# Result stores on SyncE's queue, streamed weights on GpSimd's, and the next pair's conversion placed behind the operands it follows

## The chip, the core and the metric

The kernel runs on one core of one Trainium2 chip. The metric is the time of one execution on the device in microseconds. Before the change it is 922.56 us, the median of three runs (919.75 to 926.53).

## What is computed

Local attention over chunks of 64 tokens, in fp32, and a feed-forward layer with a PReLU on its output; q, k, v are 8 x 8 x 576 x 64, so there are 4608 tokens of width 512, and the hidden width is 2048.

```python
scores = scale * np.matmul(q_c, k_c.transpose(0, 1, 2, 4, 3))      # chunks of 64 tokens
attn = np.exp(scores - np.max(scores, axis=-1, keepdims=True))
attn = attn / (np.sum(attn, axis=-1, keepdims=True) + 1e-09)
x = merge_heads(np.matmul(attn, v_c))                               # 4608 x 512
h = x @ w_in                                                        # 4608 x 2048
g = np.maximum(h, 0.0) + alpha * np.minimum(h, 0.0)
out = g @ w_out                                                     # 4608 x 512
```

## The kernel before

Every fp32 matmul is made of three passes of a reduced format (fp32r): each operand is split into a high part (a cast on ScalarE) and a low part (a subtraction on VectorE), and high x high, high x low and low x high are summed in PSUM. `split` (L541) is that cast and subtraction.

The tokens are 36 attention pieces of 128 and 9 blocks of 512. Blocks 0 to 2 are done plainly; blocks 3 to 8 in three pairs, each by a Strassen-Winograd scheme with 7 products in place of 8.

**Attention phase with plain blocks** (steps, L440; the profile to about 382 us). 48 steps, each 24 matmuls, walk over the 16 hidden slices of blocks 0 to 2, in parts: block 0 slices 0 to 3, block 1 slices 0 to 8, then the rest of block 0, of block 1, and block 2. What a part leaves unfinished is stored as a partial sum (`store`, L350, with `keep`) and added later (L369 loads it, L370 adds it on VectorE, L383 stores the result); one buffer of two halves named "more" serves the partial sums of row blocks 0, 1 and 3, so the load for row block 3 waits until the first two results have left. In this phase the weights come in (`fetch`, L116), are split (`split_weight`, L122), and at some steps a **visit** (L402) does the scores and softmax of one attention piece and the values of an earlier one; a visit ends with eight small transfers (L242) that move VectorE's block transposes "t" into the tile pT. At every odd step from 15 to 45, `combine` (L478) forms the sums of weights that the Strassen scheme needs, on VectorE and ScalarE, and `keep_a` (L474, GpSimd's queue) writes them to HBM in tiles wi_a and wo_a.

**Pairs** (L751 on). `first_product` (L591) makes 7 products with w_in for each of 8 slices j; in pairs 0 and 1 a visit stands ahead of each j, for the blocks of the next pair. `second_product` (L647) makes 7 products with w_out (order 7, 1, 5, 6, 4, 2, 3), 8 units j each, a unit being 6 matmuls; `operand` (L624) prepares the activations of a unit, two units ahead (AHEAD, L645): a difference on VectorE where the product needs one (L628, L631), and a split (L542, L543). The weights come back from HBM by `stream` (L514): 168 loads of 512 KB, two units each, into a ring of four tiles (raw, raw, wi15, wo15); the load of a tile is issued when the tile's last matmul has been placed, so it waits for TensorE. The conversion of the next pair's activations (`convert`, L545) is 14 pieces, each a split, for four of the seven products after a difference (L560, L564); `second_product` emits one piece every four units (L682).

What sets the order: a scheduler places each instruction in the queue of its engine by a simulated timeline, program order being the priority, and lifts what stands under `tc.high_priority`; TensorE's order is pinned from step 20 on. Queues run in order, and a DMA waits in the queue of the engine that issues it. SyncE's queue (SP) issues all loads (weights, q, k, v, pT, partial sums, the stream); GpSimd's queue (POOL) issues the writes of combined weights and all result stores except the very last two.

## Time and profile before

| | |
|---|---|
| median of 3 runs | 922.56 us (919.75 to 926.53) |
| the profiled execution | 921.13 us, span 919.4 us |
| TensorE matmul busy | 838.4 us, 91% of the span |
| VectorE, ScalarE, GpSimd busy | 699.1, 539.0, 115.0 us |
| mean granted TensorE clock | 0.961 |
| DMA traffic | 184.5 MB, mean 201 GB/s; 143.2 MB of it from SP's queue, 40.4 MB from POOL's |
| stages, ends | attention phase with plain blocks 382, pair 0 574, pair 1 757, pair 2 919 |

In the lines of the profile PE is TensorE, DVE VectorE, ACT ScalarE, POOL GpSimd and SP SyncE; L524 is line 524 of the kernel; "out<-in" names the tiles; the brackets at a row's end give the time that the engine stood idle before it and what ended that. A time of "x8" rows is that of eight instructions together. Busy TensorE is not TensorE at its peak: at half clock a matmul counts as twice as long, so the granted clock is to be read beside it.

### The profile page before, as it was taken

To read this page: it belongs to the slowest core of one execution; us is meant where nothing else is said; L and a number is where in the kernel's file an instruction comes from. 1 tells how busy PE (TensorE), PEld (TensorE's weight loads), DVE (VectorE), ACT (ScalarE), POOL (GpSimd) and SP (SyncE) were. 2 spreads that over 40 slices of the span, in tenths; PEclk is the share of its full clock that TensorE was granted. 3 is DMA by queue.
4 is the path that set the end of the run, shared out by engine and by line. 5 is a ranking of instruction groups with operands and counts; after the bars stand their busy time and mean duration, and the time that the engine had idled before them with its cause. 6 is when DMAs were issued, how large, how long until landed. Compare 5 with 4: busy or idle time off the path is not lost.

```text
span 919.4 us, 15294 instructions
## 1 busy us (share of the span) xinstructions
PE 838.4 (91%) x5248; PEld 661.6 (72%) x5248; DVE 699.1 (76%) x1313; ACT 539.0 (59%) x1366; POOL 115.0 (13%) x174
## 2 busy tenths in 40 slices
PE   5798999996787899998896999899979999998998
PEld 4566888775665678876674888677758888886886
DVE  6599999987878747566689985566899845678884
ACT  5676565663554756476585643667766435565542
POOL 4013232234243200000000001000000010000000
PEclk9799999998897899999998999999999999999999
DMA  9648668566666733466664567766635676554564
GB/s 286 225 132 271 198 223 268 162 207 222 237 206 211 243 99 93 152 225 219 227 196 152 181 207 232 261 191 208 225 123 184 209 236 219 183 186 161 199 207 165
DMA packets 69212, 184.52 MB, mean 201 GB/s; under 512 B 11408, under 2 KB 18576, under 8 KB 69136
## 3 DMA queue, kind: packets, MB, share of 16 engines
q1 hardware_dynamic: 56672, 143.17, 49.1%
q0 software_dynamic: 12320, 40.38, 12.2%
q8 instruction: 42, 0.69, 0.3%
q14 instruction: 34, 0.28, 0.1%
q10 hardware_dynamic: 144, 0.01, 0.0%
HBM read 135.27 MB, written 40.89 MB: 192 GB/s over the span
## 4 chain that ended last, share of the span: by engine, by line
PE 68%; DVE 10%; DMA 9%; ACT 5%; SPq 4%; issue 3%; POOL 1%; DVEq 0%; ACTq 0%; POOLq 0%
PE ps_o L677 15%; PE ps_o L586 13%; PE ps_h L319 11%; PE ps_o L343 11%; PE ps_h L677 7%; PE ps_h L586 6%; SPq L242 2%; DMA raw<-wi_a 2%; DMA wi<-wi_a 2%; DMA wo_a<-raw 1%; DMA wi_a<-raw 1%; PE ps_a L282 1%; PE ps_a L199 1%; ACT pr L223 1%; PE ps_a L185 1%
## 5 line engine op out<-in xcount | busy, mean ns | idle before, releaser
L343 PE MATMUL ps_o<-wo,gh 128*128 128x512 f32 x384 | 116.5, 402 | 15.2 <-DVE more L370 14.5
L319 PE MATMUL ps_h<-xh,wi 128*128 128x512 f32 x384 | 112.1, 416 | 1.3 <-DVE g L311 1.3
L343 PEld LDWEIGHTS ps_o<-wo,gh 128*128 128x128 f32 x384 | 73.0, 191 | 34.0 <-DVE more L370 15.4
L319 PEld LDWEIGHTS ps_h<-xh,wi 128*128 128x128 f32 x384 | 74.0, 197 | 20.2 <-DVE g L311 1.8
L586 PE MATMUL ps_o<-wi,raw 128*128 128x512 f32 x168 | 68.2, 406 | 8.7 <-DMA raw<-wi_a 8.7
L223 ACT ACTIVATE pr<-ps_a,mx 128x64 f32<-128x64 f32 x224 | 67.0, 325 | 11.5 <-DVE mx L220 11.5
L343 PE MATMUL ps_o<-wo,gl 128*128 128x512 f32 x192 | 69.8, 397 | 0.0
L586 PE MATMUL ps_o<-wo,raw 128*128 128x512 f32 x168 | 68.0, 405 | 0.0
L663 POOL DMA_DIRECT2D outT<-xl x10 | 5.4, 541 | 454.4 <-DVE xl L653 454.1
L319 PE MATMUL ps_h<-xl,wi 128*128 128x512 f32 x192 | 54.3, 402 | 0.0
L309 ACT ACTIVATE g<-ps_h 128x512 f32<-128x512 f32 x48 | 29.0, 605 | 41.5 <-PE ps_h L319 41.0
L223 ACT ACTIVATION_READ_ACCUMULATOR pr<-ps_a,mx 128x1 f32 x224 | 48.9, 218 | 0.0
L331 ACT CAST gh<-g 128x512 fp32r<-128x512 f32 x48 | 29.8, 622 | 30.7 <-DVE g L311 18.6
L309 ACT ACTIVATE wo<-gh 128x512 f32<-128x512 f32 x24 | 15.2, 635 | 52.9 <-DVE gh L609 52.9
L542 ACT CAST gh<-wi 128x512 fp32r<-128x512 f32 x48 | 30.0, 625 | 27.3 <-PE ps_o L677 12.8
L586 PEld LDWEIGHTS ps_o<-wi,raw 128*128 128x128 f32 x168 | 32.3, 192 | 17.5 <-DVE gl L618 6.2
L319 PEld LDWEIGHTS ps_h<-xl,wi 128*128 128x128 f32 x192 | 37.6, 196 | 9.3
L343 PEld LDWEIGHTS ps_o<-wo,gl 128*128 128x128 f32 x192 | 36.4, 189 | 8.8
L504 ACT CAST raw<-t 128x512 fp32r<-128x512 f32 x32 | 19.6, 629 | 32.6 <-DVE t L500 11.1
L543 DVE TENSOR_TENSOR gl<-wi,gh 128x512 fp32r<-128x512 f32 x48 | 32.9, 685 | 7.6 <-ACT gh L542 6.9
L677 PE MATMUL ps_o<-gh,wo 128*128 128x512 f32 x112 | 38.5, 403 | 0.1
L311 DVE SCALAR_TENSOR_TENSOR g<-ps_h,g 128x512 f32<-128x512 f32 x48 | 32.6, 679 | 7.8 <-ACT g L310 7.6
(250 smaller groups left out, 2254.6 us busy)
## 6 DMA issues: line engine op xcount, KB each, us to landing
raw<-wi_a SPq DMA_DIRECT2D x42, 512.0 KB, 5.3
raw<-wo_a SPq DMA_DIRECT2D x42, 512.0 KB, 3.4
wi<-wi_a SPq DMA_DIRECT2D x21, 512.0 KB, 4.4
wo<-wi_a SPq DMA_DIRECT2D x21, 512.0 KB, 4.4
wi<-wo_a SPq DMA_DIRECT2D x21, 512.0 KB, 3.3
wo<-wo_a SPq DMA_DIRECT2D x21, 512.0 KB, 3.9
wi_a<-raw POOLq DMA_DIRECT2D x32, 256.0 KB, 4.1
wo_a<-raw POOLq DMA_DIRECT2D x32, 256.0 KB, 3.4
```

The costliest lines, as they stand in the source:

```text
L223: nc.scalar.activation(pr[:, g], one, AF.Exp, bias=mx[:, g], scale=SCALE, accum_out=sm[:, g])
L242: nc.sync.dma_start(out=pT[dst, i].rearrange("p h t -> p (h t)"), in_=tb[src, j].rearrange("p h t -> p (h t)"),)
L309: nc.scalar.activation(g, h, AF.Relu, scale=-1.0)
L311: nc.vector.scalar_tensor_tensor(g, in0=h, scalar=0.0, in1=g, op0=ALU.max, op1=ALU.subtract)
L319: pe(nc.tensor.matmul(hps, lhsT=wi[f][:, l, k * P:(k + 1) * P], rhs=xx[:, k], start=(i == 0 and k == 0), stop=(i == 2 and k == NK - 1),))
L331: nc.scalar.copy(gh, g)
L343: pe(nc.tensor.matmul(o, lhsT=a[:, ts], rhs=wo[f][:, l], start=(f == first and i == 0), stop=(f == last and i == 2),))
L504: nc.scalar.copy(w[:, 0], t)
L542: nc.scalar.copy(t_hi, t)
L543: nc.vector.tensor_tensor(t_lo, t, f32(t_hi), op=ALU.subtract)
L586: pe(nc.tensor.matmul(ps, lhsT=w[:, l, k * P:(k + 1) * P], rhs=xx[:, xl], start=first and at == 0, stop=at == n - 1, skip_group_check=not ...
L677: pe(nc.tensor.matmul(ps[m], lhsT=w[:, l, m * P:(m + 1) * P], rhs=xx, start=i != 6 and j == 0 and n == 0, stop=j == JF - 1 and n == 2, ski ...
```

## The change

Four edits. Result stores (L383, L663) all go to SP's queue, and the stream of combined weights (L524) goes to POOL's. In `second_product` a conversion piece is queued, on ScalarE and on VectorE, behind the two instructions of the split made last (`tc.issue_after` orders the queue and adds no wait). The conversion's order becomes 1, 2, 7, 5, 6, 3, 4, so that the pieces with a plain split come first, and for pair 0 its first four pieces are emitted from step 40 on. The steps at which a combine is emitted come from a table instead of every odd step. The prologue of the stream is three loads ahead of the last plain matmuls and one behind, instead of two and two.

```diff
@@ store
-            (nc.sync if end else nc.gpsimd).dma_start(out=dst, in_=ob)
+            nc.sync.dma_start(out=dst, in_=ob)
@@ stream
-        nc.sync.dma_start(out=f32(t), in_=units[side][n])
+        nc.gpsimd.dma_start(out=f32(t), in_=units[side][n])
@@ split
-        nc.scalar.copy(t_hi, t)
-        nc.vector.tensor_tensor(t_lo, t, f32(t_hi), op=ALU.subtract)
+        hi = nc.scalar.copy(t_hi, t)
+        return hi, nc.vector.tensor_tensor(t_lo, t, f32(t_hi), op=ALU.subtract)
@@ convert
-        x0, x1 = x.pop(b), x.pop(b + 1)
+        x0, x1 = x[b], x[b + 1]
...
-        order = [(i, k) for i in (7, 5, 1, 6, 3, 4, 2) for k in range(2)]
+        order = [(i, k) for i in (1, 2, 7, 5, 6, 3, 4) for k in range(2)]
@@ operand
-        split(t, hi, lo)
+        behind[:] = split(t, hi, lo)
...
+    behind = []
@@ second_product
-                (nc.sync if end and (half, col) == (0, 1) else nc.gpsimd).dma_start(out=outT[rows, cols], in_=ys[:, m])
+                nc.sync.dma_start(out=outT[rows, cols], in_=ys[:, m])
...
-                    conversion.pop(0)()
+                    with tc.issue_after(behind[0].ins), tc.issue_after(behind[1].ins):
+                        conversion.pop(0)()
@@ steps
+    COMBINE = (16, 18, 20, 21, 23, 25, 27, 28, 30, 32, 34, 36, 37, 39, 41, 43)
...
-        elif n % 2 and combined:
+        elif n in COMBINE:
...
-        if n == len(steps) - 3:
+        if n == len(steps) - 8:
             ops, conversion = convert(PLAIN)
-        if n >= len(steps) - 3:
-            for _ in range(5):
+        if n >= len(steps) - 8:
+            for _ in range(1 if len(conversion) > 10 else 0 if n < len(steps) - 3 else 4):
...
-    for _ in range(2):
+    for _ in range(3):
         stream()
...
-    for _ in range(RING - 2):
+    for _ in range(RING - 3):
         stream()
```

TensorE's order stays as it was. Three places show what moves elsewhere.

SP's queue in the first product of pair 0, at the visit whose pT transfers the trace has at 414 us; raw, wi_ and wo_ are ring tiles loaded from the combined weights wi_a. Before:

```order
L242 DMA pT<-t_4393 32x256 x8
L159 DMA q_sb<-qT 128x512
L161 DMA k_sb<-kT 128x512
L168 DMA v_sb<-v 128x512
L524 DMA raw<-wi_a_373 128x1024
L524 DMA wi_4563<-wi_a_374 128x1024
L524 DMA wo_4580<-wi_a_375 128x1024
L524 DMA raw<-wi_a_376 128x1024
L242 DMA pT<-t_4542 32x256 x8
```
After:

```order
L242 DMA pT<-t_4393 32x256 x8
L159 DMA q_sb<-qT 128x512
L161 DMA k_sb<-kT 128x512
L168 DMA v_sb<-v 128x512
L242 DMA pT<-t_4542 32x256 x8
L159 DMA q_sb<-qT 128x512
L161 DMA k_sb<-kT 128x512
```
The four stream loads between two visits are gone from SP; they stand on POOL's queue, which holds nothing but the 168 stream loads from the last written piece of combined weights to its end.

SP's queue at the end of block 0 in the attention phase; "more" and "ob" are the buffers of finished row blocks and "partial" the stored sums. Before:

```order
L242 DMA pT<-t_2125 32x256 x8
L159 DMA q_sb<-qT 128x512
L161 DMA k_sb<-kT 128x512
L168 DMA v_sb<-v 128x512
L369 DMA more<-partial_3_895 128x512
L369 DMA ob<-partial_2_1460 128x512
L242 DMA pT<-t_2299 32x256 x8
L369 DMA more<-partial_0_1452 128x512
```
After:

```order
L242 DMA pT<-t_2125 32x256 x8
L159 DMA q_sb<-qT 128x512
L161 DMA k_sb<-kT 128x512
L168 DMA v_sb<-v 128x512
L383 DMA out<-more 128x512 x2
L383 DMA out<-ob 128x512
L369 DMA more<-partial_3_895 128x512
L369 DMA ob<-partial_2_1460 128x512
L242 DMA pT<-t_2299 32x256 x8
L383 DMA out<-more 128x512
```
The three stores stood on POOL before, between writes of combined weights. They now stand on SP behind the eight pT transfers and three loads of a visit, and ahead of the partial sum that needs their buffer; the fourth store stands behind the next visit's pT.

VectorE's queue at the turn from the first to the second product of pair 0. Rows of L543 that read xh or xl are conversion pieces, those that read g or wi_ after L628 and L631 are operands. Before:

```order
L543 TENSOR_TENSOR wi_5498<-xh,wi_5498 128x512
L543 TENSOR_TENSOR wo_5499<-xh,wo_5499 128x512
L618 TENSOR_TENSOR gl<-ps_h,g 128x512
L228 TENSOR_TENSOR pr<-pr,sm 128x512
L543 TENSOR_TENSOR wi_5714<-xl,wi_5714 128x512
L543 TENSOR_TENSOR wo_5715<-xl,wo_5715 128x512
L628 TENSOR_TENSOR g<-wo_4593,wi_4592 128x512
L543 TENSOR_TENSOR wi_5914<-xh,wi_5914 128x512
L235 STREAM_TRANSPOSE t_5134<-pr 128x8x2x32
L543 TENSOR_TENSOR wo_5915<-xh,wo_5915 128x512
L311 SCALAR_TENSOR_TENSOR wo_5196<-gh,wo_5196 128x512
L631 TENSOR_TENSOR wi_4592<-wi_4592 128x512
```
After:

```order
L618 TENSOR_TENSOR gl<-ps_h,g 128x512
L228 TENSOR_TENSOR pr<-pr,sm 128x512
L628 TENSOR_TENSOR g<-wo_4593,wi_4592 128x512
L311 SCALAR_TENSOR_TENSOR wo_5196<-gh,wo_5196 128x512
L235 STREAM_TRANSPOSE t_5134<-pr 128x8x2x32
L311 SCALAR_TENSOR_TENSOR wi_5195<-gl,wi_5195 128x512
L631 TENSOR_TENSOR wi_4592<-wi_4592 128x512
L311 SCALAR_TENSOR_TENSOR wo_5196<-gl,wo_5196 128x512
L543 TENSOR_TENSOR gl<-g,gh 128x512
L311 SCALAR_TENSOR_TENSOR wi_5195<-ps_o_5158,wi_5195 128x512
L543 TENSOR_TENSOR gl<-g,gh 128x512
L628 TENSOR_TENSOR g<-wo_4740,wi_4739 128x512
```
The six conversion splits left this place. In the second product a piece now stands behind the split of every fourth operand, for instance `L543 TENSOR_TENSOR wi_5288<-xh,wi_5288 128x512` behind the operand of the fourth unit ahead, and its last one near the end of the product.

## The prediction

> **What bounds the kernel now.** First I read the busy times by stage (start and end, length, then busy us and instruction counts of PE, PEld, DVE, ACT, POOL, then the granted PE clock). TensorE is the busiest engine, so time can come only from where it stands idle or runs at half clock. The stages are the late attention phase (200 to 382), the first product of pair 0 and its turn into the second (482 to 520), the same two of pair 1 (574, 660), and the second product of pair 2.
>
> ```profile
> 200.00:382.00 182.00, 155.70 (x1279) 122.79 (x1281) 131.24 (x270) 100.81 (x321) 44.99 (x66) 0.92 0.54 177
> 382.00:482.00 100.00, 92.25 (x844) 72.34 (x834) 66.99 (x131) 68.42 (x223) 1.05 (x2) 0.97 0.67 226
> 482.00:520.00 38.00, 29.52 (x107) 22.97 (x107) 36.67 (x61) 24.28 (x43) 0.00 (x0) 0.87 0.48 160
> 520.00:574.00 54.00, 54.00 (x274) 43.58 (x276) 39.72 (x63) 22.86 (x37) 3.50 (x7) 1.00 0.67 219
> 574.00:660.00 86.00, 80.71 (x715) 63.44 (x708) 56.96 (x109) 57.77 (x179) 0.82 (x2) 0.96 0.68 224
> 660.00:700.00 40.00, 34.39 (x136) 25.64 (x136) 38.29 (x65) 27.82 (x52) 0.00 (x0) 0.96 0.45 144
> 834.50:920.00 85.50, 78.68 (x337) 62.55 (x335) 61.88 (x98) 39.31 (x66) 3.24 (x6) 1.00 0.55 179
> ```
>
> PE's idle time (length less busy) is 26.3, 7.8, 8.5, 0, 5.3, 5.6 and 6.8 us. Of the last, 0.6 lies past the span's end of 919.4 and 4.5 is the final adds and stores after the last matmul (it ends at 914.9, below), so the turn of pair 2 costs about 2: there no attention and no conversion compete. Next the waits of PE in those stages (total, times, longest): first products, then turns.
>
> ```profile
> PE ps_o L586 <- DMA raw<-wi_a: 6.0, 2, 3.4
> PE ps_h L586 <- DMA wi<-wi_a: 1.7, 2, 1.5
> ...
> PE ps_o L586 <- DMA raw<-wi_a: 2.7, 1, 2.7
> PE ps_o L586 <- DMA wi<-wi_a: 2.6, 1, 2.6
> ...
> PE ps_o L677 <- DVE gl L543: 6.1, 2, 3.6
> PE ps_o L677 <- DMA raw<-wo_a: 2.3, 1, 2.3
> ...
> PE ps_h L677 <- DVE gl L543: 4.4, 3, 2.0
> ```
>
> So the first products wait for streamed weights, the turns for operand splits on VectorE. Why the weights are late stands in SyncE's timeline (start, length), and in the chain of waits:
>
> ```profile
> 414.47 5.61 SPq L242 DMA_DIRECT2D pT<-t  x8
> 421.23 0.43 SPq L168 DMA_DIRECT2D v_sb<-v  x1
> 421.70 0.43 SPq L524 DMA_DIRECT2D raw<-wi_a  x1
> ```
> ```profile
> 421.70 6.30 DMA raw<-wi_a
> 436.80 2.80 PE ps_o L586 x12
> 904.55 10.36 PE ps_h L677 x45
> ```
>
> The stream load stands behind eight pT pieces, 5.6 us of issuing that also waits for the visit's softmax, and three attention loads; once issued it needs another 6.3 us. Twelve matmuls take 2.80, so 0.233 each at full clock.
>
> **The sum, part by part,** against the profiled execution's own 921.13 us (span 919.4; the median of the runs shown is 922.56, 1.4 above).
>
> A, streams to POOL's queue. All 168 loads of 512 KB leave SP; POOL's queue has nothing else once the last combined piece is written, so no attention row stands ahead of one. Both first products stop waiting: 7.8 + 5.3 = 13.1 us idle, and half clock after the gaps, (1 - 0.97) x 100 = 3.0 and (1 - 0.96) x 86 = 3.4. Full gain 19.5. What a load costs on POOL the trace shows only for other sizes (KB each, us to landing; then busy us, mean ns and idle time of a store):
>
> ```profile
> raw<-wi_a SPq DMA_DIRECT2D x42, 512.0 KB, 5.3
> wi_a<-raw POOLq DMA_DIRECT2D x32, 256.0 KB, 4.1
> ```
> ```profile
> L663 POOL DMA_DIRECT2D outT<-xl x10 | 5.4, 541 | 454.4 <-DVE xl L653 454.1 <-issue 0.3
> ```
>
> A ring tile feeds 12 matmuls, 2.8 us, and three tiles are in hand when the fourth is freed: a load has 8.4 us. With 0.54 us of issue it needs 0.5 + 5.3 = 5.8 if landing is as on SP, 0.5 + 8.2 = 8.7 if landing doubles with the bytes. I take near 6.3: most of a short transfer is latency, and 256 KB against 512 KB differ by 1.2 us across the two queues. That is inside the 8.4, so it is hidden; a few loads under attention traffic will still be late. A is 17 (bounds -17, landing at 8.7 as the second rival works out, to 19.5).
>
> B, conversion behind the operands. VectorE's timeline at the turn of pair 0, and the matmul that waits there:
>
> ```profile
> 481.59 0.64 DVE L543 TENSOR_TENSOR wi<-xh,wi 128x512 fp32r<-128x512 f32 x1
> 482.15 0.68 DVE L543 TENSOR_TENSOR wo<-xh,wo 128x512 fp32r<-128x512 f32 x1
> ...
> 486.99 0.65 DVE L543 TENSOR_TENSOR wo<-xh,wo 128x512 fp32r<-128x512 f32 x1
> 490.56 1.29 DVE L543 TENSOR_TENSOR gl<-g,gh 128x512 fp32r<-128x512 f32 x2
> ```
> ```profile
> 491.30 0.80 PE L677 MATMUL ps_o<-gl,raw 128*128 128x512 f32 x1 [3.60 <-DVE gl L543]
> ```
>
> Six conversion splits lie between 481.59 and 487.6, starts 0.60 apart, so the operand at 490.56 comes 3.6 us late, just what PE waits. The order after the change has none of the six there. The two turns cost 8.5 + 5.6 idle and (1 - 0.87) x 38 = 4.9 and (1 - 0.96) x 40 = 1.6 of clock, 20.6 in all. About 2 stays at each, as in pair 2, and 1 at each for the last visit's softmax: -6. Then the moved work must fit later: 14 splits and 8 differences a pair, 22 x 0.60 = 13.2 us of VectorE, one piece each four units. Cover: 520 to 574 leaves VectorE 54 - 39.7 = 14.3. The tight place is the middle (products 5, 6, 4; 24 units, 33.6 us of PE): 24 splits, 16 differences, 10 adds and 12 moved instructions, 62 x 0.60 = 37.2, 3.6 too much, of which the two operands ahead cover 2.8. I charge 1 a pair. B is 20.6 - 6 - 2 = 12.6, say 13 (bounds 2, the fourth rival, to 18). ScalarE's 14 casts a pair fit: it is busy 22.9 of 54.
>
> C, stores to SP in the attention phase. Timelines of POOL, SP and PE at the end of block 0, then of block 1:
>
> ```profile
> 208.06 1.12 POOL L383 DMA_DIRECT2D out<-more  x2
> 220.86 0.57 POOL L383 DMA_DIRECT2D out<-more  x1 [9.21 <-DVE more L370]
> ...
> 271.21 1.25 POOL L383 DMA_DIRECT2D out<-more  x2
> ```
> ```profile
> 205.77 7.96 SPq L242 DMA_DIRECT2D pT<-t  x8
> 215.48 0.33 SPq L369 DMA_DIRECT2D more<-partial  x1
> ...
> 275.42 0.33 SPq L369 DMA_DIRECT2D more<-partial  x1
> ```
> ```profile
> 220.61 1.22 PE L343 MATMUL ps_o<-wo,gh 128*128 128x512 f32 x2 [8.18 <-DVE more L370]
> 239.86 0.47 PE L282 MATMUL ps_a<-pT,v_sb 64*64 64x64 f32 x2 [4.29 <-ACT pr L223]
> 279.62 1.22 PE L343 MATMUL ps_o<-wo,gh 128*128 128x512 f32 x2 [6.36 <-DVE more L370]
> ```
> ```profile
> 237.51 0.62 ACT L504 CAST raw<-t 128x512 fp32r<-128x512 f32 x1 [1.80 <-DMA wi_a<-raw]
> ```
> ```profile
> 268.77 0.69 DVE L505 TENSOR_TENSOR raw<-t,raw 128x512 fp32r<-128x512 f32 x1 [3.54 <-ACT raw L504]
> 270.11 1.28 DVE L370 TENSOR_TENSOR more<-ps_o,more 128x512 f32<-128x512 f32 x2
> ```
>
> PE waits for the add of the fourth row block; the add needs its partial sum, whose load needs the buffer that the first stores empty. Block 0: the stores went at 208.06 on POOL, and the load at 215.48, behind pT. On SP the stores themselves come after that pT and the loads behind it, at 215.4, and land in about 4 (the 4.1 of a 256 KB store above), so the load goes some 4 us later: a loss of 4. But POOL no longer stands 9.21 us at 220.86 with combined pieces behind it; they held the buffers that ScalarE's cast waited for at 237.51, and with it the softmax and PE's 4.29: a gain of up to 5. Block 1: the stores followed the adds of 270.11 at once, so POOL did not hold them; the adds were late by the 3.54 us that VectorE waited on a cast. There I count 0. Of the half clock, (1 - 0.92) x 182 = 14.6 in the stage, I count 1. C is -4 + 5 + 1 = 2 (bounds: -8 if the loss of 4 comes at both blocks and nothing is gained; +14 if, with POOL free, half of the 26.3 goes). The new place of the combines in the table moves few rows of VectorE: 0. Queued behind a waiting store on SP are the next visit's loads, due a visit (11 us) later.
>
> D, the other stores: pairs 0 and 1 put theirs on SP at the end of the second product, ahead of loads that are due only after the next visit; the last was on SP already. 0.
>
> Sum: A 17 + B 13 + C 2 = 32; 921.1 - 32 = 889, and with the median's 1.4 about 890.
>
> **Rivals.**
> 1. The streams stay late. For it: DMA is busy 0.67 to 0.68 in both first products, and 6.3 us to land is long. Against: in the second products, without pT, the share is the same 0.67 at 520 to 574 and PE is never idle. A is then 0: 890 + 17 = 907. The Trainium skill has this as a rule: "DMA: Bandwidth & Descriptors", section on issuing engines that are not separate DMA queues, says that transfers from all engines share the same DMA engines and that spreading them saves only the usually small issue time; by that rule it is 907. The trace's 5.61 us of issue per visit speaks against "small".
> 2. The other side: POOL's loads are too slow for the ring. Place: L524 on POOL; point: issue to landing over 8.4 us. At 9.5 each tile takes 9.5/3 = 3.17 instead of 2.8, so 168 x 0.37 = 62 us more; with no A, 907 + 62 = 969; at 8.7 each tile takes 2.9, the loss is 17 and the time 924. It is slower by over 1% from about 8.8 on. For it: 4.1 us for half the bytes. Against: 541 ns an issue, with VectorE near full in the same stages. The Trainium skill, "SBUF — State Buffer", section on two separate sides, warns that VectorE in a two-port mode can keep GpSimd from writing descriptors; no row here shows an issue held up so.
> 3. Phase 200 to 382 loses: the stores and the loads that wait for them hold up SP at both block ends, C = -8: 900.
> 4. VectorE becomes the bound of the second products: the 3.6 too much comes whole, with ScalarE's cast ahead of each moved split, so B = 2: 901.
> 5. All of it is given back by waits elsewhere: 922.
>
> **How the numbers follow.** Forecast (all three parts near their size) 0.52; rivals 1: 0.14, 2: 0.06, 3: 0.10, 4: 0.13, 5: 0.05. Predicted time 890. The range 869 to 911 takes in rivals 1, 3 and 4 and the runs' spread above them; its lower end is all three parts at their upper bounds, 922.5 - 19.5 - 18 - 14 = 871, less 2 for that spread. A measurement can tell about 1%, 9 us. Faster: forecast and rivals 1, 3, 4 make 0.89, less some overlap, 0.87; same 0.07 (rival 5 and part of 2); slower 0.06.
>
> **What would show it.** A: the first products of pairs 0 and 1 without PE waits on wi_a loads, clock 1.00, L524 on POOL landing under 7 us. B: no conversion split between the turn's operands, PE idle at each turn 2 to 4 us, none over 1 us in the middle. C: the wait on L370 longer at block 0, shorter at block 1, ScalarE waiting less for wi_a writes. Wrong: waits of PE on raw or wi loads in second products (rival 2), or waits on gl and more splits in the middle (rival 4).

## The result, and the profile after

The changed kernel takes 891.74 us (median of four runs, 889.24 to 893.51) against 921.7 (919.75 to 926.53) for the kernel before: a ratio of 0.9665, 95% interval 0.9619 to 0.9711. The forecast was 890, range 869 to 911. The total came out where the sum put it; its three terms did not.

To see where the time went I cut both profiled executions at the same events, the first matmul of each product, and not at round times. Length of each stage in us; the first row is the time at which pair 0 starts, which is the length of the attention phase with the plain blocks. The differences were taken before rounding:

| stage | before | after | difference |
|---|---|---|---|
| start of pair 0 | 382.8 | 375.8 | -7.0 |
| pair 0, first product | 101.7 | 89.8 | -12.0 |
| pair 0, second product | 90.0 | 87.5 | -2.5 |
| pair 1, first product | 95.3 | 87.6 | -7.6 |
| pair 1, second product | 86.4 | 86.2 | -0.2 |
| pair 2, first and second | 78.4, 81.1 | 78.4, 81.1 | 0 |

The first products of the changed kernel, pair 0 and then pair 1, and the second products behind each (start and end, length, busy us and count of PE, PEld, DVE, ACT, POOL, then clock, DMA share, GB/s):

```profile
375.83:465.58 89.75, 88.52 (x791) 69.44 (x785) 65.22 (x128) 66.27 (x220) 14.27 (x27) 1.00 0.79 255
465.58:553.08 87.50, 81.28 (x401) 64.79 (x399) 76.84 (x125) 48.83 (x83) 15.31 (x29) 0.98 0.60 196
553.08:640.69 87.61, 87.02 (x728) 68.69 (x722) 63.14 (x118) 62.67 (x190) 14.26 (x27) 1.00 0.73 237
640.69:726.90 86.21, 80.99 (x337) 63.75 (x336) 73.81 (x119) 47.61 (x82) 14.80 (x28) 0.98 0.58 190
```

Both first products run at full clock (1.00), PE is busy to within 1.2 and 0.6 us of their length, and no wait on a streamed load is left. The longest wait of PE in the first product of pair 0 is now:

```profile
PE ps_o L586 <- ACT g L607: 0.5, 1, 0.5
```

The stream's loads on GpSimd's queue, first the issuing (count, busy us, mean ns, then the idle time ahead), then the landing (KB, median us from issue to landing):

```profile
L524 POOL DMA_DIRECT2D raw<-wo_a x42 | 22.2, 528 | 109.3 <-PE ps_o L678 62.6
L524 POOL DMA_DIRECT2D raw<-wi_a x42 | 22.3, 530 | 102.1 <-PE ps_o L586 61.1
```
```profile
raw<-wi_a POOLq DMA_DIRECT2D x42, 512.0 KB, 4.1
raw<-wo_a POOLq DMA_DIRECT2D x42, 512.0 KB, 3.6
```

GpSimd stands idle ahead of the loads because the ring is full and it waits for matmuls: the loads are early. 0.53 + 4.1 = 4.6 us is far inside the 8.4 us that the ring gives.

The second products still stop. PE's stalls in that of pair 0, the first two at the turn, the last two in the middle:

```profile
471.59 0.50 PE L678 MATMUL ps_o<-gl,raw 128*128 128x512 f32 x1 [2.88 <-DVE gl L543]
480.61 0.50 PE L678 MATMUL ps_o<-gl,wo 128*128 128x512 f32 x1 [1.61 <-DVE gl L543]
520.53 0.50 PE L678 MATMUL ps_o<-gl,raw 128*128 128x512 f32 x1 [0.99 <-DVE gl L543]
522.92 0.50 PE L678 MATMUL ps_o<-gl,raw 128*128 128x512 f32 x1 [0.74 <-DVE gl L543]
```

And VectorE's timeline ahead of the first of them:

```profile
468.45 0.70 DVE L235 STREAM_TRANSPOSE t<-pr 128x512 f32<-128x512 f32 x1
469.09 0.64 DVE L311 SCALAR_TENSOR_TENSOR wi<-gl,wi 128x512 f32<-128x512 f32 x1
469.65 0.67 DVE L631 TENSOR_TENSOR wi<-wi 128x512 f32<-128x512 f32 x1
470.25 0.68 DVE L311 SCALAR_TENSOR_TENSOR wo<-gl,wo 128x512 f32<-128x512 f32 x1
470.86 0.68 DVE L543 TENSOR_TENSOR gl<-g,gh 128x512 fp32r<-128x512 f32 x1
```

No conversion split stands there any more, as forecast. But VectorE has no gap: the last visit's softmax, the PReLU of the last slice (L311) and a difference that product 5 needs only two products later (L631) stand ahead of the split that PE waits for. In the attention phase (170 to 382) PE's waits, before and then after (total, times, longest):

```profile
PE ps_o L343 <- DVE more L370: 14.5, 2, 8.2
PE ps_a L282 <- ACT pr L223: 8.9, 6, 4.3
```
```profile
PE ps_o L343 <- DVE more L370: 16.8, 2, 10.8
PE ps_a L282 <- DMA k_sb<-kT: 3.0, 1, 3.0
PE ps_a L282 <- ACT pr L223: 2.6, 3, 1.3
```

Read by stages alone, the stream was worth 19.6 us, the conversion 2.7 and the stores 7.0. That was my first reading, with the fourth rival (VectorE the bound, conversion worth 2) as the explanation. The experiments show that it is wrong.

### The profile page after: what moved, and what is told of

It is laid out like the page before. It is cut to its first block, busy times and chain, and to the rows that moved or that the text cites. A ratio compares the mean times of both kernels' runs of the same rounds, so it can differ in the third digit from the quotient of the medians.

```text
span 890.9 us, 15308 instructions
## 1 busy us (share of the span) xinstructions
PE 823.7 (92%) x5248; PEld 650.7 (73%) x5248; DVE 698.6 (78%) x1313; ACT 537.6 (60%) x1366; POOL 179.6 (20%) x300
## 4 chain that ended last, share of the span: by engine, by line
PE 62%; DVE 17%; DMA 10%; ACT 6%; issue 2%; SPq 2%; POOL 0%; DVEq 0%; ACTq 0%
PE ps_o L678 14%; PE ps_o L586 12%; PE ps_h L319 10%; PE ps_o L343 10%; PE ps_h L586 6%; PE ps_h L678 6%; DMA wi<-kT 2%; SPq L242 2%; DVE wi L631 2%; DVE gl L543 1%; DMA k_sb<-kT 1%; ACT pr L223 1%; DMA wo_a<-raw 1%; DMA wi_a<-raw 1%; DMA v_sb<-v 1%
## 5 line engine op out<-in xcount | busy, mean ns | idle before, releaser
L319 PE MATMUL ps_h<-xh,wi 128*128 128x512 f32 x384 | 109.3, 407 | 1.3 <-DVE g L311 1.3
L319 PEld LDWEIGHTS ps_h<-xh,wi 128*128 128x128 f32 x384 | 72.2, 192 | 19.6 <-DVE g L311 1.8
L524 POOL DMA_DIRECT2D raw<-wo_a x42 | 22.2, 528 | 109.3 <-PE ps_o L678 62.6
L524 POOL DMA_DIRECT2D raw<-wi_a x42 | 22.3, 530 | 102.1 <-PE ps_o L586 61.1
L543 DVE TENSOR_TENSOR gl<-wi,gh 128x512 fp32r<-128x512 f32 x48 | 32.7, 684 | 11.8 <-ACT gh L542 11.0
L332 DVE TENSOR_TENSOR gl<-g,gh 128x512 fp32r<-128x512 f32 x48 | 32.8, 683 | 7.9 <-ACT gh L331 7.1
L586 PEld LDWEIGHTS ps_o<-wi,raw 128*128 128x128 f32 x168 | 31.6, 188 | 9.3 <-ACT g L607 2.1
L311 DVE SCALAR_TENSOR_TENSOR g<-ps_h,g 128x512 f32<-128x512 f32 x48 | 32.6, 679 | 7.1 <-ACT g L310 6.9
```

What stands on the lines that cost most here:

```text
L311: nc.vector.scalar_tensor_tensor(g, in0=h, scalar=0.0, in1=g, op0=ALU.max, op1=ALU.subtract)
L319: pe(nc.tensor.matmul(hps, lhsT=wi[f][:, l, k * P:(k + 1) * P], rhs=xx[:, k], start=(i == 0 and k == 0), stop=(i == 2 and k == NK - 1),))
L332: nc.vector.tensor_tensor(gl, g, f32(gh), op=ALU.subtract)
L524: nc.gpsimd.dma_start(out=f32(t), in_=units[side][n])
L543: return hi, nc.vector.tensor_tensor(t_lo, t, f32(t_hi), op=ALU.subtract)
L586: pe(nc.tensor.matmul(ps, lhsT=w[:, l, k * P:(k + 1) * P], rhs=xx[:, xl], start=first and at == 0, stop=at == n - 1, skip_group_check=not ...
```

## The experiments

All runs in one table: the start of pair 0 and the stage lengths come from the one profiled execution of each kernel, the median and the ratio to the kernel before (95% interval) from the timed runs, 4 to 10 of each. The first product of pair 2 is 78.4 everywhere, its second 81.1 to 81.2, and 78.6 and 78.4 in the last two. The steps of the combines, the prologue of the stream and the four early pieces were not run by themselves.

| kernel | start of pair 0 | first, second of pair 0 | first, second of pair 1 | median | ratio |
|---|---|---|---|---|---|
| before | 382.8 | 101.7, 90.0 | 95.3, 86.4 | 922 to 925 | 1 |
| after | 375.8 | 89.8, 87.5 | 87.6, 86.2 | 891.74 | 0.9665 (0.9619 to 0.9711) |
| stream alone | 381.8 | 89.8, 94.5 | 87.6, 88.2 | 907.29 | 0.9841 (0.9783 to 0.9898) |
| conversion alone | 383.7 | 104.1, 83.8 | 95.6, 84.0 | 912.60 | 0.9876 (0.9813 to 0.9938) |
| stores alone | 374.5 | 102.9, 91.1 | 94.4, 87.2 | 918.47 | 0.9951 (0.9926 to 0.9976) |
| after, free pieces | 380.6 | 89.8, 89.1 | 87.6, 85.3 | 897.29 | 0.9715 (0.9676 to 0.9755) |
| after again | 375.6 | 89.8, 87.5 | 87.6, 84.6 | 892.16 | 0.9656 (0.9613 to 0.9698) |
| before, pT on GpSimd | 378.0 | 91.1, 93.9 | 88.0, 91.2 | 905.19 | 0.9783 (0.9736 to 0.9830) |
| after, low left out | 378.0 | 89.8, 85.3 | 87.6, 81.1 | 887.65 | 0.9595 (0.9554 to 0.9636) |
| after, low on GpSimd | 378.7 | 89.8, 88.2 | 87.6, 88.6 | 898.25 | 0.9720 (0.9677 to 0.9763) |
| after, old stores | 385.4 | 89.8, 87.5 | 87.6, 84.6 | 899.01 | 0.9722 (0.9683 to 0.9761) |
| slots | 380.1 | 89.8, 84.8 | 87.6, 81.5 | 887.48 | 0.9587 (0.9541 to 0.9633) |
| slots and differences | 375.3 | 90.0, 86.8 | 87.6, 80.7 | 884.85 | 0.9576 (0.9544 to 0.9609) |
| own tile | 378.5 | 89.9, 84.9 | 87.6, 80.7 | 884.82 | 0.9574 (0.9537 to 0.9611) |

### Each part by itself

**The stream alone**, in the kernel before:

```diff
-        nc.sync.dma_start(out=f32(t), in_=units[side][n])
+        nc.gpsimd.dma_start(out=f32(t), in_=units[side][n])
```

> The kernel before with one edit: the stream of combined weights (L524) on GpSimd's queue; stores and conversion as before. My theory: on SyncE's queue each load stood behind a visit's eight pT issues, so both first products lose all their waits on wi_a and their half clock: 19 us, and the second products stay as before (89 to 90 and 86 to 87 us): 921.7 - 19 = about 903, first products 89 to 90 and 87 to 88 us. Rival: the gain of the first products came partly with the conversion's new places and the longer prologue, so the loads alone bring about half: 911, first products still above 92. Second rival: the pair's result stores, which here stand on the same queue ahead of the next loads, hold the stream up at the end of each second product: first products gain 19, the second lose 2 to 4 each, about 908.

The first products lose their 11.9 + 7.6 = 19.5 us, just as in the changed kernel. But the second products get 4.5 + 1.8 = 6.3 longer, so the edit is worth 13.2 by the stages and 923.2 - 907.3 = 15.9 by the medians (interval 9 to 20), not 17 to 19. The size is that of the second rival of this expectation; its cause, the stores on the same queue, is refuted further below. What the traces show in its place stands in the counts of VectorE. The first and second product of pair 0, before and then with the stream alone:

```profile
382.78:484.48 101.70, 91.60 (x790) 71.63 (x784) 68.98 (x134) 70.90 (x228) 0.54 (x1) 0.97 0.68 228
484.48:574.44 89.96, 83.82 (x400) 66.92 (x400) 74.06 (x119) 44.66 (x75) 3.78 (x7) 0.94 0.58 190
```
```profile
381.80:471.60 89.80, 88.54 (x791) 69.41 (x785) 65.24 (x128) 67.05 (x221) 15.15 (x29) 1.00 0.79 258
471.60:566.09 94.49, 84.53 (x402) 67.10 (x400) 77.69 (x125) 48.12 (x82) 18.94 (x36) 0.93 0.56 181
```

The DVE counts go from 134 and 119 to 128 and 125: six instructions that VectorE used to finish while PE waited for weights now lie behind the turn. Six times 0.60 is 3.6 us, and the stall at the turn grew from the 3.60 of the prediction's row by 3.5, as PE's timeline with the stream alone shows:

```profile
481.83 0.79 PE L677 MATMUL ps_o<-gl,raw 128*128 128x512 f32 x1 [7.08 <-DVE gl L543]
```

PE's wait for weights had been VectorE's time to catch up. Taking the wait away moved part of it to the next stage. Pair 1 agrees: there the counts go from 122 and 116 to 119 and 119, three instructions or 1.8 us, and its second product gets 1.8 us longer.

**The conversion alone**, in the kernel before (the order of the pieces, and each piece queued behind the last split):

```diff
-        order = [(i, k) for i in (7, 5, 1, 6, 3, 4, 2) for k in range(2)]
+        order = [(i, k) for i in (1, 2, 7, 5, 6, 3, 4) for k in range(2)]
...
-                    conversion.pop(0)()
+                    with tc.issue_after(behind[0].ins), tc.issue_after(behind[1].ins):
+                        conversion.pop(0)()
```

> The kernel before with one edit: each conversion piece queued behind the operand split made last, and the new order of the pieces; queues as before. My theory: VectorE is full at the turn and again in products 5, 6 and 4, so the stall only moves: the second products of pairs 0 and 1 gain 2 to 4 us together, 918 to 920 in all. Rival: the edit is worth the 13 us that the prediction gave it, and in the changed kernel something else (loads on GpSimd's queue, stores on SyncE's) took 10 back: about 909, second products 83 to 84 us. Second rival: the first products need the new places of the pieces too, so it comes out 5 to 8 us faster with the gain in the first products.

My theory of 2 to 4 us fell here. The second products go to 83.8 and 84.0, 6.1 + 2.4 = 8.5 less; the first products, where PE still waits for loads, give 2.7 of it back, and no run here shows why. By the medians it is 10.6 (interval 6 to 17; its runs lie between 907.5 and 916.6, and the profiled one is the longest). Its stalls in the second product of pair 0:

```profile
487.75 1.66 PE L678 MATMUL ps_o<-t,raw 128*128 128x512 f32 x6 [2.67 <-DMA raw<-wo_a]
494.25 1.44 PE L678 MATMUL ps_o<-t,wi 128*128 128x512 f32 x5 [0.51 <-DVE t L543]
499.06 0.50 PE L678 MATMUL ps_o<-gl,wo 128*128 128x512 f32 x1 [1.75 <-DVE gl L543]
```

The 2.88 of the changed kernel is not among them. The likely reading is the same exchange seen from the other side: while PE waited 2.67 us for a load ahead of the product, VectorE got its splits done. With the stream moved as well, from "stream alone" to "after", the second products go from 94.5 and 88.2 to 87.5 and 86.2: 9.0. Of the 7.0 in pair 0, 3.7 are idle time of PE, and 3.3 are busy time, at a granted clock of 0.98 in place of 0.93. Against the second execution of the changed kernel, whose second products ran at 1.00, it is 10.6. That step holds the stores, the steps of the combines and the prologue too; the stores undone, below, leave the second products as they are, the other two were not separated. So in the second products the conversion is worth 8.5 without the stream, and about 9 to 10.6 with it. In the stages of the changed kernel it shows as 2.7, because the stream's edit had put 6.3 there.

**The stores alone**, in the kernel before:

```diff
-            (nc.sync if end else nc.gpsimd).dma_start(out=dst, in_=ob)
+            nc.sync.dma_start(out=dst, in_=ob)
...
-                (nc.sync if end and (half, col) == (0, 1) else nc.gpsimd).dma_start(out=outT[rows, cols], in_=ys[:, m])
+                nc.sync.dma_start(out=outT[rows, cols], in_=ys[:, m])
```

> The kernel before with one edit: all result stores on SyncE's queue; stream, conversion and the table of combines as before. My theory: the attention phase gains the 5 to 6 us that the changed kernel gained there, because GpSimd's combined pieces no longer stand behind a store, minus the later load of the partial sum at block 0: first matmul of pair 0 at about 377 instead of 383, total 915 to 917. Rival: the stores only delay the partial sums, and the changed kernel's gain there came from the new steps of the combines: 0 to 4 us slower, 922 to 926, with ScalarE still waiting for a combined piece near 237. Second rival: the stream, still on SyncE here, is held behind the stores at the ends of the second products: 1 to 3 us of loss there.

It is 4.7 us faster by the medians (interval 2.2 to 6.8), a little less than expected. By the stages 8.3 us are gained ahead of pair 0 and 2.3 given back in the pairs, the size that the second rival named; the profiled execution is the fastest of the ten. The waits are those of the changed kernel:

```profile
PE ps_o L343 <- DVE more L370: 16.2, 2, 10.4
PE ps_a L282 <- DMA k_sb<-kT: 3.7, 1, 3.7
PE ps_a L282 <- ACT pr L223: 2.3, 3, 1.2
```

PE waits longer for the partial sums (14.5 before) and much less for the softmax (8.9 before). No change in the steps of the combines was needed for that. The three parts by their medians make 15.9 + 10.6 + 4.7 = 31.2; the whole change made 30.0 in its own comparison and 31.6 in the second one. They add up, within intervals of several us each.

**The stores undone**, in the changed kernel (the two lines above turned round):

> The changed kernel with one edit undone: the result stores (L383, L663) go through GpSimd's queue again, with the stream behind them there. My theory: the attention phase loses the 5 us that the stores alone gained, because combined pieces stand behind stores again and ScalarE waits for their buffers; the first matmul of pair 0 goes from 376 to about 381, and at the ends of the second products the stream waits for the last adds, 0 to 2 us: 896 to 899. Rival: the attention phase's gain came from the new steps of the combines: 891 to 893. Second rival: the stores hold the stream up for good at the ends of the second products, the next first products wait for raw and wi loads 3 us and more each: 900 to 905.

It loses 899.0 - 892 = 7 us; in the profiled executions all of the loss lies ahead of pair 0 (385.4 against 375.6), with the waits of the kernel before:

```profile
PE ps_o L343 <- DVE more L370: 13.6, 2, 7.3
PE ps_a L282 <- ACT pr L223: 9.0, 6, 2.4
```

The second products are the same 87.5 and 84.6 as in the second execution of the changed kernel, with stores and stream on one queue. So it was not the stores that lengthened the second products of "stream alone".

### Why the stream gained, and what it gave back

**pT on GpSimd's queue**, in the kernel before, the stream left on SyncE's:

```diff
-                    nc.sync.dma_start(
+                    nc.gpsimd.dma_start(
                         out=pT[dst, i].rearrange("p h t -> p (h t)"),
```

> The kernel before with one edit: the pT pieces (L242) go through GpSimd's queue, the stream stays on SyncE's. My theory: what made the loads late is only that they stood behind pT, so this does in the first products what moving the stream did: 90 and 88 us in place of 102 and 95, and the second products get 4 to 5 and 2 us longer, as they did with the stream alone: about 905 to 908, if the attention phase stays as it was. Rival: GpSimd's queue is the faster way for the stream as such: first products stay above 97 and 92, total 915 or more. Second rival: in the attention phase pT now stands behind combined pieces that wait, and it gets 3 to 6 us longer there: 910 to 913.

First products 91.1 and 88.0, second 93.9 and 91.2, 905.2 us: near the theory's numbers, but for the second product of pair 1, 4.8 us longer and not 2, at a granted clock of 0.94 in place of 0.98. The stream was on the queue where it always was. What made the loads late is their place behind pT, and not SyncE's queue as such. This version has a price of its own: its first matmul of pair 0 waits 10.9 us for the first streamed load, and its attention phase (378.0) has that in it. The last combined pieces leave GpSimd only at 366.9 (312.7 before), and the first two stream loads, which use the same "raw" tiles, go out at 368.5 and 373.4 (315.9 and 319.3 before). Without that wait TensorE would have reached pair 0 at 367.1, 15.7 us earlier than before and ahead of every other version here; PE waits less there on L370 (11.3 in place of 14.5) and hardly on the softmax (0.7 in place of 8.9). No run joins that gain with a stream that is loaded early enough.

**Less work for VectorE.** In the changed kernel ScalarE copies the piece a second time where VectorE subtracted:

```diff
+    def spare(t, t_hi, t_lo):
+        nc.scalar.copy(t_hi, t)
+        nc.scalar.copy(t_lo, t)
...
-            split(t, ops[i, k][:, 0], ops[i, k][:, 1])
+            (spare if beside_pairs[0] else split)(t, ops[i, k][:, 0], ops[i, k][:, 1])
```

> The changed kernel with part of the work left out: in the second products the low half of each conversion piece is not subtracted on VectorE; ScalarE copies the piece a second time in its place, so the values are not the reference's. VectorE loses 14 x 0.6 = 8.4 us in each of the two second products, ScalarE gains as much. Theory (VectorE's backlog, carried from the first product into the turn and met again in products 5, 6 and 4, sets the stalls): second products of pairs 0 and 1 fall from 87.5 and 86.2 to 83 to 85, total 885 to 888. Rival (the stalls come from the chain cast, subtraction, matmul of single operands and from where the scheduler put them, not from VectorE's load): within 1 us of the changed kernel, 891 to 893, or slower by the casts on ScalarE.

887.65 against 892.16 for the changed kernel on the same chip; the second products go to 85.3 and 81.1 from 87.5 and 84.6. VectorE is busy 8.2 and 8.0 us less there; that gives PE 2.3 and 3.5 back, though ScalarE is busy some 6 us longer in each. So VectorE's load does set part of the stalls, but a microsecond less for VectorE is not one less for PE; and the first stall of the turn in pair 0 stays at 2.9.

**The same subtractions on GpSimd**, with all of the work done (`nc.gpsimd.tensor_tensor(t_lo, t, f32(t_hi), op=ALU.subtract)` for the second copy above):

> The changed kernel with the same 14 subtractions of each pair done on GpSimd, so all of the work is there. Theory: if a subtraction on GpSimd takes 1 to 2 us, the stream loads behind it still land inside the 8.4 us that the ring has, and VectorE gains its 8.4 us: second products 84 to 86, total 886 to 889. Rival: GpSimd's queue stands still at each subtraction until ScalarE's cast is done, the loads behind it come too late, and PE waits on wo_a loads in the second products again: 895 to 905. Second rival: GpSimd and VectorE slow one another, VectorE's subtractions get longer than 0.6 us: no gain, 891 to 895.

898.25: slower than the changed kernel by 6. The mechanism is that of the second rival, though the time lies outside its 891 to 895. In the profiled executions 4.6 us lie in the second products and 3.1 ahead of pair 0. Groups of the subtractions on GpSimd (L549), and of the splits on VectorE:

```profile
L549 POOL TENSOR_TENSOR wi<-xl,wi 128x512 fp32r<-128x512 f32 x8 | 20.5, 2561 | 2.7 <-ACT wi L548 2.7
L549 POOL TENSOR_TENSOR wo<-xl,wo 128x512 fp32r<-128x512 f32 x8 | 10.3, 1290 | 1.8 <-ACT wo L548 1.7
...
L543 DVE TENSOR_TENSOR gl<-wi,gh 128x512 fp32r<-128x512 f32 x48 | 38.9, 813 | 13.4 <-ACT gh L542 13.4
L543 DVE TENSOR_TENSOR gl<-wo,gh 128x512 fp32r<-128x512 f32 x24 | 21.7, 903 | 6.0 <-ACT gh L542 5.8
```

In the changed kernel those two groups of VectorE have means of 684 and 686 ns. No wait on a stream load came back. VectorE has 14 instructions fewer in each second product, and nearly the same busy time (75.7 against 76.8 us in pair 0).

**The pieces placed by the scheduler again**, in the changed kernel:

```diff
-                    with tc.issue_after(behind[0].ins), tc.issue_after(behind[1].ins):
-                        conversion.pop(0)()
+                    conversion.pop(0)()
```

> The changed kernel with one edit undone: the conversion pieces are again placed by the scheduler and not queued behind the operand's split; their new order stays. My theory: the placement itself is worth what the second products gained, 2 to 3 us: about 894 to 895, stalls of 3 to 4 us at the turns again and fewer in products 5, 6 and 4. Rival: the placement is worth the predicted 13 and the changed kernel lost 10 of it to VectorE being full elsewhere, which remains: about 903 to 905. Second rival: the scheduler places them no worse, because the new order begins with the cheap pieces: 892, within 1 us.

**The changed kernel a second time**, unedited:

> The changed kernel once more, unedited, beside the other kernels of this call. The version with free pieces came 5.6 us above it, yet its second products were only 0.8 us longer together; 4.7 lie ahead of pair 0, where the two have the same order on every engine. If that part is only the scatter between executions and chips, this run comes to 894 to 898, and the placement of the pieces is worth 1 to 3. If the placement is worth the 5.6, it stays at 889 to 893.

Free pieces cost 5 us in the median (897.3 against 891.7 and 892.2), none of the three expectations of that kernel holds, and the second execution says that the 5 us are no mere scatter between chips. Yet the second products account for only 174.5 against 173.7 and 172.1, so 0.8 to 2.4; of the 9 to 10.6 on top of the stream little is thus in the placement. Most is in the rest, and there the other order of the pieces is the likely part: "conversion alone" has the order and gains 8.5 without the early pieces, the new steps of the combines or the longer prologue. What the placement changes is where PE stops: with free pieces one stall of 7.1 us at the turn of pair 0 is back, as long as with the stream alone, and those in the middle shrink from 0.99 and 0.74 to 0.23 and 0.64. The other 5 lie ahead of pair 0, where every engine has the same instructions in the same order in both kernels. The nine executions here with all stores on SyncE's queue reach pair 0 between 374.5 and 380.6 us, four with the stores on GpSimd's (and pT on SyncE's) between 381.8 and 385.4. The means, 377.4 and 383.4, are 6.0 apart, which is the steadier figure for the stores. Why a kernel lies high or low in its band stays open.

### Two versions that go further

If VectorE's load over a stretch sets the stalls, the conversion pieces belong where it has time: the six adds of product 6 come where each unit needs a difference and a split already.

```diff
-                if conversion and j % 4 == 3:
+                if conversion and (i == 1 and j < 6 or i in (2, 3) and j % 2):
```

> The changed kernel with the 14 conversion pieces of a pair at other places: six in product 1 (one a unit) and four each in products 2 and 3 (one every two units), none in products 7, 5, 6 and 4, where VectorE is full. The amount of work is the same. Theory (VectorE's load over a stretch sets the stalls): the stalls in products 5, 6 and 4 (1.7 us of PE a pair) go and the second stall at the turn gets shorter; second products 85 and 83 to 84, total 887 to 889. Rival (the stalls are the price of single chains, or the pieces now come too late for the next first product): 891 to 895, with waits for conversion tiles at the start of the next pair.

887.48. Its stalls in the second product of pair 0, all of them:

```profile
475.94 0.50 PE L678 MATMUL ps_o<-gl,raw 128*128 128x512 f32 x1 [2.88 <-DVE gl L543]
484.36 0.50 PE L678 MATMUL ps_o<-gl,wo 128*128 128x512 f32 x1 [0.81 <-DVE gl L543]
```

The two in the middle are gone and the second at the turn is half; the first is the same 2.88. With the same work as the changed kernel it gains what leaving the subtractions out gained (887.48 and 887.65). The first products lose nothing: the late pieces are in time.

```diff
             one, two = {5: (b12, b11), 6: (b22, b12), 4: (b21, b12)}[i]
-            nc.vector.tensor_tensor(b12, one, two, op=ALU.subtract)
+            with tc.issue_after(splits[-4].ins):
+                nc.vector.tensor_tensor(b12, one, two, op=ALU.subtract)
```

> As the version with other slots, and the eight differences of product 5, which the scheduler lifts up to the turn (five of them stand among the operands that PE waits for), are queued behind the split of four units earlier. Theory: the turn loses 2 to 3 us of VectorE's work ahead of the awaited splits; the stalls there go from 2.9 and 1.6 us to under 2 and under 0.5, second products of pair 0 at 83 to 84 and of pair 1 at 82 to 83: 884 to 887. Rival: the differences are then late for product 5, where each unit needs a difference, a cast and a split in its 1.4 us, and the stall only moves there: no better than the slots alone, 887 to 892.

884.85, the best together with the version after it; against the slots alone pair 1 gains 0.7 and pair 2 2.6, but pair 0 loses 1.9. Its stalls there:

```profile
471.70 0.80 PE L680 MATMUL ps_o<-gl,raw 128*128 128x512 f32 x1 [3.27 <-DVE gl L543]
521.90 0.51 PE L680 MATMUL ps_o<-gl,raw 128*128 128x512 f32 x1 [1.34 <-DVE gl L543]
```

The differences are no longer ahead of the awaited split, and the stall is no shorter: it was not their load that held it. They are also a little late in the middle (1.34), as the rival said. My next theory: what holds the first split is its tile, since "gl" has two buffers and the last slice holds both until its PReLU. The operands of the third and fourth unit get tiles of their own:

```diff
-        if at % 4 == 1:
+        if at in (2, 3):
+            both = const.tile([P, 2, TB], F32R, name=rooms[at - 2])
+            hi, lo = both[:, 0], both[:, 1]
+        elif at % 4 == 1:
```

> As the version with slots and differences, and the operands of the third and fourth unit at a turn get two tiles of their own (rooms of the first product's operands of product 5, read for the last time early in its last slice) in place of the gp tiles gh and gl. Theory: the stall of 3.3 us that is left at the turn is no longer a matter of VectorE's load alone; the third unit's split has its cast done 6 us before, but its tile gl is held by the last slice until that slice's PReLU. With a tile of its own the split stands eight instructions earlier (8 x 0.6 = 4.8 us) and the stall goes to under 1 us: second product of pair 0 at 82 to 84, total 880 to 883. Rival (VectorE's load alone): the stall moves to the fifth and sixth unit, whose splits stand behind the same PReLU, and the second product keeps 86 us: 884 to 886.

PE's stalls in the second product of pair 0:

```profile
473.34 0.50 PE L683 MATMUL ps_o<-wo,raw 128*128 128x512 f32 x1 [0.65 <-ACT wo L542]
474.27 1.43 PE L683 MATMUL ps_o<-wo,raw 128*128 128x512 f32 x5 [0.42 <-DVE wo L543]
479.92 0.50 PE L683 MATMUL ps_o<-gl,wo 128*128 128x512 f32 x1 [0.38 <-DVE gl L543]
523.07 0.51 PE L683 MATMUL ps_o<-gl,raw 128*128 128x512 f32 x1 [1.34 <-DVE gl L543]
```

The stall of 3.27 breaks up into 0.65, 0.42 and 0.38, so the tile was what held it: the third unit's split now runs at 468.0, 1.4 us after its cast began, where it stood 7.4 us behind it (463.6 to 471.0) as long as the last slice had the tile. VectorE was busy nearly throughout with what was queued ahead of that split, which is why the trace alone looked like a matter of load. The second product of pair 0 gains 1.9 (86.8 to 84.9), no more, and the median is the same 884.8: the 880 to 883 did not come. In the profiled execution the start of pair 0 is 3.1 later, inside the band named above, so a gain of that size can't be told from these runs. Both versions beat the changed kernel by 7 us.

## Why the prediction came out, point by point

**What bounds it.** PE waited where the prediction said, for the loads in the first products and for splits in the second. That holds.

**A, 17 us; measured 13 to 16.** The waits and the half clock of the first products went whole, the 19.5 that the prediction named as the upper bound. A load needs 0.53 + 4.1 = 4.6 us from issue to landing and not the 6.3 that I took; the 256 KB writes were no guide to it. The failed step is the one that is not there: the sum ends at the first product's end. It never asks what VectorE did in those 13 us of waiting, and 6.3 us came back at the next turn.

**B, 13 us; measured 8.5 to 10.6 in the second products.** The mechanism is right in the main: no conversion split stands among the operands of a turn, and with either placing of the stream the second products are shorter for it. Mis-sized are two terms. "About 2 stays at each, as in pair 2, and 1 at each for the last visit's softmax: -6": the stalls left at the two turns are 4.5 and 3.4 us, 7.9. "I charge 1 a pair" for VectorE in the middle: it is 0.99 + 0.74 in each pair, 3.5 in all. Those of pair 0 stand in the section on the result; PE's timeline of the changed kernel in pair 1, four at the turn and two in the middle:

```profile
646.35 0.50 PE L678 MATMUL ps_h<-gl,raw 128*128 128x512 f32 x1 [0.75 <-DVE gl L543]
650.57 1.43 PE L678 MATMUL ps_h<-more,wi 128*128 128x512 f32 x5 [1.14 <-DVE more L543]
653.75 0.50 PE L678 MATMUL ps_h<-gh,wo 128*128 128x512 f32 x1 [0.35 <-ACT gh L542]
655.38 0.50 PE L678 MATMUL ps_h<-gl,wo 128*128 128x512 f32 x1 [1.13 <-DVE gl L543]
695.51 0.50 PE L678 MATMUL ps_h<-gl,raw 128*128 128x512 f32 x1 [0.99 <-DVE gl L543]
697.91 0.50 PE L678 MATMUL ps_h<-gl,raw 128*128 128x512 f32 x1 [0.74 <-DVE gl L543]
```

Together that is 1.9 + 1.5 = 3.4 too little, and 13 - 3.4 = 9.6. The stalls in the middle are where the prediction put them, as the version with other slots shows by removing them. What the prediction has no word of is the tile "gl": the 2.88 at the turn of pair 0 stays when VectorE has less to do (2.9) and when the pieces go elsewhere (2.88), and among the versions of the changed kernel it breaks up only when the operand gets a tile of its own.

**C, 2 us; measured 4.7 alone, 7 undone.** The step for block 0 held in its direction: -4 forecast, and the longest wait on L370 goes from 8.2 to 10.8, so -2.6. The softmax gave 6.3 (8.9 to 2.6) where 5 was put. Too small is the 1 for the clock. Two windows that the stage fills, before and then after:

```profile
200.00:250.00 50.00, 36.83 (x318) 28.94 (x317) 40.81 (x88) 26.11 (x91) 18.48 (x27) 0.86 0.70 235
250.00:300.00 50.00, 41.25 (x333) 32.28 (x332) 40.82 (x87) 24.22 (x72) 19.57 (x28) 0.90 0.60 202
```
```profile
200.00:250.00 50.00, 37.87 (x328) 29.69 (x328) 41.38 (x90) 26.41 (x85) 15.13 (x21) 0.90 0.71 238
250.00:300.00 50.00, 43.53 (x411) 34.06 (x410) 41.84 (x87) 26.38 (x85) 17.78 (x25) 0.93 0.66 216
```

(0.90 - 0.86) x 50 + (0.93 - 0.90) x 50 = 3.5 us, by windows that hold somewhat different work. A wait of 3.0, which the profile puts down to a k load, is new and was not forecast; that load was issued on SyncE at 305.6, behind eight pT pieces.

**D, 0.** The end after the last matmul is 0.8 us longer (5.24 against 4.45) with the stores all on one queue; with the stores undone it is the old length again.

**The sum.** 17 + 13 + 2 = 32 against 13 + 9 + 7 = 29 by the stages. A and B were too large by 4 each and C too small by 5, so that the total came within 2 us is luck in part: errors of both signs, each of a few us.

**The rivals.** The first (streams stay late, 907) is refuted by both ways of taking them from behind pT. The Trainium skill, "DMA: Bandwidth & Descriptors", section "Issuing engines are not separate DMA queues", would have only a usually small issue time saved by a second issuing engine; here the first products gained 19.5 us, and what it freed was the place behind pT in an in-order queue. The second (ring too slow) is refuted by the 4.1 us. The third fell with the sign of C. The fourth described real stalls (0.99 + 0.74), but its price, B = 2, seemed to come true only in the plain comparison of stages; the edit by itself takes 8.5 off the second products.

## What to carry to other kernels

A difference between stages before and after a change of several parts tells where the time went, not which part did it: here one part's gain lay in the stage that another part had lengthened, and only runs of each part alone could separate them. Before you count a removed wait in full, ask which engine used it to catch up, and count its instructions on both sides of the next hand-over. And when a stall stays the same after work was moved out of its way, look for the buffer that its first instruction waits for.

## What the runs showed of the hardware

GpSimd is no free second VectorE for fp32 subtractions on 128x512 tiles: one took 1.29 to 3.09 us in the means of its groups (two of them are shown with that run), and VectorE's splits beside it went from 684 and 686 to 813 and 903 ns. VectorE's adds that read one operand from PSUM did not slow down (683 ns in the changed kernel too); in the version with GpSimd:

```profile
L660 DVE TENSOR_TENSOR xl<-ps_o,xl 128x512 f32<-128x512 f32 x16 | 10.8, 683 | 4.0 <-PE ps_o L684 4.0
```

The Trainium skill, "SBUF — State Buffer", section "Who interferes with whom", has it that a VectorE instruction with two inputs in SBUF contends with a GpSimd instruction that reads SBUF; these rows agree with it. Loads issued by GpSimd, on the other hand, were not held up beside a nearly full VectorE: 528 to 530 ns an issue in the mean, and 569 at most, in the changed kernel, where VectorE was busy for all of the 10 us from 465 to 475.
